# A small tile of 128 bytes becomes one of 512 bytes, and two thirds of the on-chip memory moves up by 384 bytes

## The chip, the cores and the metric

The kernel runs on one core of a Trainium2 chip. The metric is the device time of one launch in microseconds (us). The engines are named as the profile names them: PE is TensorE's matmul, PEld its load of the stationary operand, DVE is VectorE, ACT is ScalarE, POOL is GpSimd and SP is the engine that issues most DMAs. SBUF is the on-chip memory: 128 partitions, in each of which a tile takes the same range of bytes. A byte address below always means the address inside a partition.

## The reference

Pooled attention feeds a gated feed-forward layer.

```python
q, k, v: (8, 8, 576, 64) float32          # batch, heads, sequence, head size
k_p = k.reshape(B, H, 72, 8, D).mean(axis=3)      # 72 pooled keys per head
v_p = v.reshape(B, H, 72, 8, D).mean(axis=3)
scores = (q @ k_p.T) / sqrt(D)
attn = softmax(scores)                            # with 1e-9 added to the sum
x = (attn @ v_p) as (4608 tokens, 512)
gate = sigmoid(x @ w_gate)                        # w_gate, w_val: (512, 1536) float64
out = (gate * (x @ w_val)) @ w_out                # w_out: (1536, 512) float64
```

The weights are float64. The kernel turns them into float32 on the chip and multiplies in three terms: each float32 operand is split into a high part that fits TensorE's one-pass fp32 form and a low rest, and high x high, high x low and low x high are summed in PSUM.

## The kernel before

**Tiling.** The 4608 tokens are nine blocks of 512. Block 0 goes through a first pass of its own, with its order of work written out by hand (`ORDER`, line 264 of the trace). Blocks 1 to 8 go in four pairs, n = 1 to 4, whose order is a list of numbers (`LATER`, line 263). Line numbers of the trace are therefore those of the two loops that issue the work, and tile names tell the operations apart.

**A pair of blocks.** The two matrix products of the feed-forward layer are each cut in 2 x 2 quarters and done with seven products instead of eight. For the first one, seven combinations of x (tiles `xo1` to `xo7`, `parts_of`, line 719) meet seven combinations of the weights (tiles `parts`, reloaded from DRAM into six rotating rooms). `SLOTS` (line 48) fixes the order of 14 products for one pair of weight columns: G1 G5 V4 G6 G2 G3 G7 V1 V5 G4 V6 V2 V3 V7, where V4 belongs to the pair of columns before. The digit says which `xo` is used. Each product is six matmuls, with 512 columns of x streaming through the array (`rhs`) against 128 x 128 of the weights (`lhsT`), `product`, line 772:

```python
t, w, x = bank[kind, b], parts.pop((kind, p, m)), xo[m]
        nc.tensor.matmul(
            t, lhsT=w[:, h, a], rhs=x[:, y, c],
```

The trace calls these matmuls `chain<-xo,parts`. The second product (`second_sums`, line 964) works in the same way on 21 units of 12 matmuls, `acc<-hs,oparts`: `oparts` are reloaded weights in three rotating rooms, and `hs` are combinations of the gated values, which reuse the rooms of the `xo` tiles. The order of these rooms is

```python
ROOMS = (1, 5, 6, 2, 3, 7, 4)
room = ROOMS[i] if i < 7 else (3, 7, 4)[(i - 7) % 3]
```

for the units i = 0 to 20. The attention of the next two blocks (scores `sc`, transposes `tp`, products with v `av`) is threaded between these matmuls in many short pieces.

**The first pass** uses `xo1` and `xo2` for its products (`whole`, line 813: 288 matmuls, trace line 264), and 144 matmuls `acc<-oparts,hs` in which the streaming and the stationary operand are the other way round.

**Where tiles lie.** Tiles come from pools, and a pool lays its rooms one behind the other in SBUF, in the order of their first use. Most tiles are multiples of 512 bytes. A few small ones are rounded up to `LINE` = 32 numbers, 128 bytes:

```python
LINE = 32
zs = work.tile([P, LINE], F32, name="zs")
```

`zs`, the row sums of the softmax, is the first of these in its pool, at byte 74752 = 146 x 512. What follows it starts 128 bytes past a multiple of 512, with few exceptions. In the built program the rooms that matter are:

| room | operand of | before | remainder by 512 | after | remainder |
|---|---|---|---|---|---|
| xo4 | streams x, hs | 12800 | 0 | 12800 | 0 |
| s1 (also an hs) | first pass | 41984 | 0 | 41984 | 0 |
| xo3, xo6, xo7 | streams x, hs | 50176, 58368, 66560 | 0 | the same | 0 |
| xo5, xo1, xo2 | streams x, hs | 76928, 85120, 93312 | 128 | 77312, 85504, 93696 | 0 |
| six rooms of parts | stationary weights | 121984 + 4096 i | 128 | 122368 + 4096 i | 0 |
| three rooms of oparts | stationary weights | 146560 + 4096 i | 128 | 146944 + 4096 i | 0 |

Inside a tile every 512-column operand and every 128 x 128 block starts at a multiple of 512 bytes from the tile's start, so the remainder of the room is that of each operand. By it the 512-column matmuls of one execution fall into two kinds, counted in the built program: in 1404 both operands have the same remainder (1332 of them 128, 72 of them 0, the first pass's `whole` among the former), and in 2064 the remainders differ (1992 with the streaming operand at 0 and the weights at 128, 72 the other way round).

Of the kernel before, what the change touches and what calls it, by code (L numbers as in the profile page):

```python
# [11 lines left out]
F32 = mybir.dt.float32  # L12
# [7 lines left out]
P = 128  # L20
# [11 lines left out]
QT = BT // P  # L32
HT = QT // 2
RING = 5
LINE = 32
# [240 lines left out]
def attention_then_ffn(ctx: ExitStack, tc: tile.TileContext, qT, kT, vm, vr, vn, sums8, wgv, wo, const, out, outT):  # L276
# [3 lines left out]
    def sb(name, bufs=1):  # L280
        return ctx.enter_context(tc.tile_pool(name=name, bufs=bufs))

    cpool, work, two = sb("cpool"), sb("work"), sb("two", 2)
# [20 lines left out]
    def behind(instruction, other):  # L304

        if book.open:
            instruction.behind = other
            return
        link(instruction, other)
# [231 lines left out]
    def load(*what):  # L541
        return fill(rawp.tile([P, S], F32, name="raw"), *what)
# [12 lines left out]
    def prep_k(b, p):  # L555
        ks = work.tile([P, KEYS + LINE - KEYS % LINE], F32, name="ks")[:, :KEYS]
        pool(ks, load("k", b, p), nc.vector)
        i = slot(b, p)
        nc.scalar.activation(kbd[i][:D, :KEYS], ks[:D], AF.Copy, scale=SCALE)
        nc.scalar.activation(kbd[i][D:, KEYS:], ks[D:], AF.Copy, scale=SCALE)  # L560

    def prep_v(b, p, eng):
        vs = work.tile([P, D], F32, name="vs")
        pool(vs, load("v", b, p), eng)
        i = slot(b, p)
        for r in (slice(0, D), slice(D, P)):
            nc.scalar.copy(vh[i][r, r], vs[r])
            eng.tensor_tensor(out=vl[i][r, r], in0=vs[r], in1=vh[i][r, r].bitcast(F32), op=ALU.subtract)

    def prep_vres(b, g, eng):  # L570
        vs = work.tile([P, D], F32, name="vs")[:96]
        pool(vs, load("r", b, g), eng)
        vc = work.tile([96, D], F32R, name="vrc")
        nc.scalar.copy(vc, vs)
        eng.tensor_tensor(out=vc[64:96], in0=vs[64:96], in1=vc[64:96].bitcast(F32), op=ALU.subtract)
        return vc

    def place_vres(b, p, vc):
        for hd in range(2):
            k = p % 2 * 2 + hd  # L580
            nc.scalar.activation(
                vres[slot(b, p)][:, hd * D:hd * D + D], vc.bitcast(F32), AF.Copy, scale=mask[:96, k:k + 1]
            )


    def segments(j):

        t0, cuts = j * BT, []
        t = t0
        while t < t0 + BT:  # L590
            b = t // S
            e = min(t0 + BT, (b + 1) * S)
            cuts.append((t - t0, e - t0, b))
            t = e
        return cuts
# [6 lines left out]
    def room_for_x(j):  # L602
        xs[side(j)] = work.tile([P, NC, BT], F32, name=f"xs{side(j)}")

    def score_matmuls(sc, q, segs, p, hf):
        with book.unit():
            for i in range(HT):
                for a, z, b in segs:
                    t = (hf * HT + i) * P
                    lo, hi = max(a, t), min(z, t + P)  # L610
                    if lo < hi:
                        nc.tensor.matmul(
                            sc[lo - t:hi - t, i], lhsT=q[:, lo:hi], rhs=kbd[slot(b, p)], start=True, stop=True
                        )

    def av_matmuls(av, ph, pl, pr, segs, p):
        for a, z, b in segs:
            i = slot(b, p)
            terms = ((vh[i], ph), (vh[i], pl), (vl[i], ph), (vres[i], pr))
            with book.unit():  # L620
                for k, (w, x) in enumerate(terms):
                    nc.tensor.matmul(av[:, a:z], lhsT=w, rhs=x[:, a:z], start=(k == 0), stop=(k == len(terms) - 1))

    def rest_of(e, rz):

        rest = work.tile([P, 4 * QT, KR], F32, name="rest")
        nc.vector.tensor_tensor(
            out=rest, in0=e.rearrange("p n i k -> p (n i) k")[:, :, KM:],
            in1=rz.rearrange("p n i -> p (n i)")[:, :, None].broadcast_to([P, 4 * QT, KR]), op=ALU.mult,
        )  # L630
        restf = rest.rearrange("p (n i h) k -> p i n (h k)", n=2, h=2)
        r3 = work.tile([P, QT, 3, 4 * KR], F32R, name="r3")
        r3v = [r3[:, :, t].rearrange("p i (n k) -> p i n k", n=2) for t in range(3)]
        nc.vector.tensor_copy(r3v[0], restf)
        end = nc.vector.tensor_tensor(out=r3v[1], in0=restf, in1=r3v[0].bitcast(F32), op=ALU.subtract)
        return (r3v[2], restf), r3, end

    def attention(j, g):
        veng = nc.vector
        segs = segments(j)  # L640
        new = [b for _, _, b in segs if (b, g) not in prepared]
        prepared.update((b, g) for b in new)
        pairs = (2 * g, 2 * g + 1)

        def room_for(shape, name):
            return ps.tile(shape, F32, name=name, tag="sc" if name == "sc" else "tp")

        e = work.tile([P, 2, 2 * QT, KEYS], F32, name="e")
        zs = work.tile([P, LINE], F32, name="zs")[:, :4 * QT].rearrange("p (n i) -> p n i", n=2)
        for n, p in enumerate(pairs):  # L650
            q = load("q", j, p)
            for b in new:
                prep_k(b, p)
            for hf in range(2):
                sc = room_for([P, HT, 2 * KEYS], "sc")
                score_matmuls(sc, q, segs, p, hf)
                scv = sc.rearrange("p i (h k) -> p (i h) k", h=2)
                m = two.tile([P, LINE], F32, name="m")[:, :QT]
                nc.vector.reduce_max(out=m, in_=scv, axis=AX.X, negate=j in BIASED)
                if j in BIASED:  # L660
                    for i in range(QT):
                        nc.scalar.activation(e[:, n, QT * hf + i], scv[:, i], AF.Exp, bias=m[:, i:i + 1])
                else:
                    nc.vector.tensor_tensor(
                        out=e[:, n, QT * hf:QT * hf + QT], in0=scv, in1=m[:, :, None].broadcast_to([P, QT, KEYS]),
                        op=ALU.subtract,
                    )
                yield
        if j not in BIASED:
            nc.scalar.activation(e, e, AF.Exp)  # L670
        nc.vector.reduce_sum(out=zs, in_=e, axis=AX.X)
        nc.vector.tensor_scalar(out=zs, in0=zs, scalar1=EPS, scalar2=float(POOL), op0=ALU.add, op1=ALU.mult)
        rz = work.tile([P, LINE], F32, name="rz")[:, :4 * QT].rearrange("p (n i) -> p n i", n=2)
        nc.vector.reciprocal(out=rz, in_=zs)
        yield
        again, r3, end = rest_of(e, rz)
        nc.scalar.copy(*again)
        tp = room_for([P, BT], "tp")
        tr = tp.bitcast(F32R)
        with book.unit():  # L680
            for i in range(QT):
                nc.tensor.transpose(out=tr[:96, i * P:(i + 1) * P], in_=r3[:, i].rearrange("p t k -> p (t k)"), identity=identr)
        pr = work.tile([96, BT], F32R, name="pr")
        nc.scalar.copy(pr, tp[:96])
        vcs = [(b, prep_vres(b, g, veng)) for b in new]

        def vprep(n, p):
            for b in new:
                prep_v(b, p, veng)
            for b, vc in vcs:  # L690
                place_vres(b, p, vc)

        for n, p in enumerate(pairs):
            pm = work.tile([P, 2 * QT, KM], F32, name="pm")
            behind(nc.gpsimd.tensor_tensor(
                out=pm, in0=e[:, n, :, :KM], in1=rz[:, n, :, None].broadcast_to([P, 2 * QT, KM]), op=ALU.mult
            ), end)
            tp = room_for([P, BT], "tp")
            pmv = pm.rearrange("p (i h) k -> p i (h k)", h=2)
            with book.unit():  # L700
                for i in range(QT):
                    nc.tensor.transpose(out=tp[:, i * P:(i + 1) * P], in_=pmv[:, i], identity=ident)
            ph = work.tile([P, BT], F32R, name="ph")
            pl = work.tile([P, BT], F32R, name="pl")
            nc.scalar.copy(ph, tp)
            nc.vector.tensor_tensor(out=pl, in0=tp, in1=ph.bitcast(F32), op=ALU.subtract)
            vprep(n, p)
            yield
            av = room_for([P, BT], "av")
            av_matmuls(av, ph, pl, pr, segs, p)  # L710
            if p == 0:
                room_for_x(j)
            nc.scalar.copy(xs[side(j)][:, p], av)
            yield
# [695 lines left out]
```

## Time and profile before

| what | value |
|---|---|
| median of 3 runs | 953.01 us (952.88 to 1102.57) |
| the profiled execution | 953.71 us, its span 951.9 us |
| PE busy | 922.8 us, 97% of the span, 4284 matmuls |
| DVE, ACT, POOL busy | 691.1 us, 572.5 us, 70.9 us |
| matmuls `chain` and `acc`, 128x512 | 2028 + 1008 + 288 + 144 = 3468 |
| mean granted TensorE clock | 0.993 |

Matmuls are pipelined: one starts about 230 ns after the one before it, while the profile gives each a length of about 395 ns, from its start to the modelled end of its last column. The step from start to start is what matters for the time. In a row of the timeline or of the chain of waits, a run of n matmuls is merged: in the timeline its length is n - 1 steps and the length of the last matmul, in the chain of waits it is n steps.

### The profile page before, as it was taken

The page shows a single profiled execution, that of the slowest core. Times are in us where ns is not written, and L with a number is a line of the kernel's source. Part 1 is how long each engine was busy: PE and PEld are TensorE (multiplying, and loading weights), DVE is VectorE, ACT ScalarE, POOL GpSimd, SP SyncE. Part 2 cuts the span into 40 slices and gives each one's busy share as a digit, 9 for nine tenths or more (in the row PEclk, how much of TensorE's full clock was granted, in tenths as well). Part 3 has the DMA queues.
Part 4 walks back from the last instruction along what each step waited for, and adds up shares of the span by engine and source line. Part 5 has one row for each costly group of instructions (what it writes and reads, how often), then busy time and mean ns, then how long its engine had stood idle before and what let it go on. Part 6 is the DMA issues. An engine that isn't in the chain of part 4 may idle for free.

```text
span 951.9 us, 12498 instructions
## 1 busy us (share of the span) xinstructions
PE 922.8 (97%) x4284; PEld 749.4 (79%) x4284; DVE 691.1 (73%) x1036; ACT 572.5 (60%) x1041; POOL 70.9 (7%) x95
## 2 busy tenths in 40 slices
PE   5899999999999999999999999999999999999997
PEld 4677878778778888888888878888888888888886
DVE  5999998877879988996439868754478663443853
ACT  6898897698898765674345646652245452233342
POOL 2011110021212100000000000000000100000000
PEclk9899999999999999999999999999999999999999
DMA  9979788757666785699555667556554665554355
GB/s 352 353 236 331 263 323 325 252 182 270 205 249 225 238 252 184 227 321 324 181 194 193 198 229 259 194 168 195 188 178 155 221 229 201 173 202 158 107 180 199
DMA packets 88494, 216.82 MB, mean 228 GB/s; under 512 B 9328, under 2 KB 28016, under 8 KB 86896
## 3 DMA queue, kind: packets, MB, share of 16 engines
q1 hardware_dynamic: 83312, 197.68, 61.2%
q0 software_dynamic: 5120, 18.35, 4.9%
q8 instruction: 34, 0.56, 0.2%
q14 instruction: 28, 0.23, 0.1%
HBM read 165.67 MB, written 50.33 MB: 227 GB/s over the span
## 4 chain that ended last, share of the span: by engine, by line
PE 69%; DVE 6%; ACT 5%; DMA 3%; issue 1%; SPq 0%; DVEq 0%; ACTq 0%
PE chain L263 41%; PE acc L263 22%; PE av L263 2%; PE sc L263 2%; ACT L263 2%; DMA oparts<-keptS 1%; PE tp L263 1%; DVE y L263 1%; DVE s L263 1%; DMA w<-keptwV 1%; DVE parts L263 1%; DMA oparts<-keptO 1%; ACT gate L263 1%; ACT e L263 1%; DVE h L263 1%
## 5 line engine op out<-in xcount | busy, mean ns | idle before, releaser
L263 PE MATMUL chain<-xo,parts 128*128 128x512 f32 x2028 | 486.9, 396 | 2.8 <-DVE o L264 1.9
L263 PEld LDWEIGHTS chain<-xo,parts 128*128 128x128 f32 x2028 | 377.5, 188 | 87.6 <-DVE o L264 2.4
L263 PE MATMUL acc<-hs,oparts 128*128 128x512 f32 x1008 | 247.2, 397 | 2.6 <-DMA oparts<-keptS 2.0
L263 PEld LDWEIGHTS acc<-hs,oparts 128*128 128x128 f32 x1008 | 186.5, 188 | 45.8 <-issue 2.4
L263 DVE TENSOR_TENSOR y<-chain,sV 128x512 f32<-128x512 f32 x69 | 47.4, 689 | 74.0 <-PE chain L263 72.5
L263 ACT COPY sG<-chain 128x512 f32<-128x512 f32 x69 | 40.4, 588 | 99.6 <-PE chain L263 99.5
L263 DVE TENSOR_TENSOR hs<-h,hs 128x1024 fp32r<-128x1024 f32 x48 | 59.4, 1237 | 33.3 <-ACT hs L263 33.2
L263 ACT CAST hs<-h 128x1024 fp32r<-128x1024 f32 x48 | 50.4, 1050 | 43.1 <-PE acc L263 42.3
L263 DVE TENSOR_TENSOR y<-chain,sG 128x512 f32<-128x512 f32 x69 | 47.1, 687 | 34.8 <-ACT gate L263 17.3
L264 PE MATMUL chain<-xo,parts 128*128 128x512 f32 x288 | 69.0, 394 | 0.9 <-DVE parts L264 0.4
L263 ACT ACTIVATE gate<-y 128x512 f32<-128x512 f32 x69 | 43.4, 632 | 37.3 <-DVE y L263 37.0
L264 PEld LDWEIGHTS chain<-xo,parts 128*128 128x128 f32 x288 | 53.3, 188 | 13.8 <-DVE parts L264 1.9
L263 ACT CAST hs<-s 128x1024 fp32r<-128x1024 f32 x36 | 37.8, 1050 | 42.6 <-PE acc L263 22.2
L263 POOL TENSOR_TENSOR pm<-e,rz 128x512 f32<-128x512 f32 x24 | 30.2, 1257 | 433.1 <-PE tp L263 169.6
L263 ACT ACT_TABLE_LOAD x44 | 56.5, 1283 | 8.9 <-DVE e L263 7.9
L263 ACT COPY sV<-chain 128x512 f32<-128x512 f32 x69 | 40.4, 587 | 21.2 <-PE chain L263 20.4
L263 DVE TENSOR_TENSOR hs<-s,hs 128x1024 fp32r<-128x1024 f32 x36 | 46.4, 1288 | 6.3 <-ACT hs L263 6.2
L263 DVE TENSOR_TENSOR h<-y,gate 128x512 f32<-128x512 f32 x69 | 48.2, 701 | 1.7
L263 DVE TENSOR_TENSOR h<-chain,gate 128x512 f32<-128x512 f32 x23 | 15.9, 690 | 39.1 <-PE chain L263 39.1
L264 PE MATMUL acc<-oparts,hs 128*128 128x512 f32 x144 | 36.6, 401 | 0.9 <-DVE oparts L264 0.8
L263 PE MATMUL sc<-kbd,raw 128*128 128x144 f32 (+1 forms) x216 | 33.6, 293 | 0.0
L263 PEld LDWEIGHTS sc<-kbd,raw 128*128 128x128 f32 (+1 forms) x216 | 28.4, 177 | 6.2 <-issue 1.9
(213 smaller groups left out, 1108.2 us busy)
## 6 DMA issues: line engine op xcount, KB each, us to landing
oparts<-keptS SPq DMA_DIRECT2D x48, 512.0 KB, 3.9
oparts<-keptO SPq DMA_DIRECT2D x72, 256.0 KB, 3.5
raw<-in_wgv SPq DMA_DIRECT2D x12, 1024.0 KB, 8.3
out<-o SPq DMA_DIRECT2D x36, 256.0 KB, 4.5
raw<-in_kT SPq DMA_DIRECT2D x28, 288.0 KB, 4.2
raw<-in_qT SPq DMA_DIRECT2D x29, 256.0 KB, 3.8
raw<-in_vm SPq DMA_DIRECT2D x24, 256.0 KB, 3.5
raw_o<-in_wo SPq DMA_DIRECT2D x12, 512.0 KB, 6.7
```

The costliest lines, as they stand in the source:

```text
L263: return self._book.take(lambda: f(*args, **named))
L264: return f(*args, **named)
```

## The change

`zs` in `attention` gets four times `LINE`, 128 numbers or 512 bytes, of which it uses the first 16 numbers as before. Everything that lies behind it in SBUF moves up by 384 bytes, and so the operands of all 512-column matmuls begin at multiples of 512 bytes. The memory's last tile ends at byte 228864 instead of 228480. The number of instructions, their kinds, and their order on each engine stay as they are; only addresses differ.

```diff
         e = work.tile([P, 2, 2 * QT, KEYS], F32, name="e")
-        zs = work.tile([P, LINE], F32, name="zs")[:, :4 * QT].rearrange("p (n i) -> p n i", n=2)
+        zs = work.tile([P, 4 * LINE], F32, name="zs")[:, :4 * QT].rearrange("p (n i) -> p n i", n=2)
         for n, p in enumerate(pairs):
             q = load("q", j, p)
```

## The prediction

> **What bounds the kernel now.** I read the page's busy times first, then busy times by stretch, the waits of PE, the chain of waits, and last the timeline of single runs of matmuls.
>
> ```profile
> span 951.9 us, 12498 instructions
> PE 922.8 (97%) x4284; PEld 749.4 (79%) x4284; DVE 691.1 (73%) x1036; ACT 572.5 (60%) x1041; POOL 70.9 (7%) x95
> L263 PE MATMUL chain<-xo,parts 128*128 128x512 f32 x2028 | 486.9, 396 | 2.8 <-DVE o L264 1.9
> L263 PE MATMUL acc<-hs,oparts 128*128 128x512 f32 x1008 | 247.2, 397 | 2.6 <-DMA oparts<-keptS 2.0
> L264 PE MATMUL chain<-xo,parts 128*128 128x512 f32 x288 | 69.0, 394 | 0.9 <-DVE parts L264 0.4
> L264 PE MATMUL acc<-oparts,hs 128*128 128x512 f32 x144 | 36.6, 401 | 0.9 <-DVE oparts L264 0.8
> ```
>
> PE is busy for 97% of the span, and the four groups of 512-column matmuls, 3468 in all, carry 840 us of its 923. The next view gives busy times by stretch; the columns are the stretch, its length, and for each engine its busy time and number of instructions, then the granted clock and DMA load.
>
> ```profile
> 0.00:60.00 60.00, 45.69 (x211) 36.37 (x212) 47.85 (x87) 48.35 (x117) 7.25 (x23) 0.91 0.92 327
> 60.00:300.00 240.00, 231.49 (x1100) 186.44 (x1099) 207.79 (x349) 208.84 (x406) 38.57 (x53) 0.99 0.73 263
> 300.00:500.00 200.00, 199.56 (x953) 163.38 (x952) 152.53 (x231) 113.34 (x212) 12.37 (x9) 1.00 0.70 239
> 500.00:700.00 200.00, 198.85 (x943) 163.14 (x942) 135.69 (x204) 101.02 (x172) 8.77 (x8) 1.00 0.62 202
> 700.00:880.00 180.00, 180.00 (x798) 146.59 (x798) 104.14 (x127) 74.50 (x107) 3.96 (x3) 1.00 0.57 190
> ```
>
> From 300 us on PE is idle for less than 1%, while DVE and ACT have room. The waits of PE after 300 us, with their sum, number and longest, say the same:
>
> ```profile
> PE acc L263 <- DMA oparts<-keptS: 2.0, 2, 1.2
> PE acc L263 <- ACT vh L263: 0.3, 1, 0.3
> ```
>
> So after 300 us the time is the number of matmuls times the step from one start to the next. Before 300 us DVE and ACT are busy for 87% and PE loses 8.5 us after the first 60: a mixed bound.
>
> **What the step depends on.** The change moves addresses alone, so the question is whether a step depends on them. The kernel itself holds the experiment, since its operands stand in all four combinations of remainders by 512. Four runs of 18 matmuls each, from the timeline of PE (start, length, count); nothing interrupts them:
>
> ```profile
> 68.00 4.25 PE L264 MATMUL acc<-oparts,hs 128*128 128x512 f32 x18
> 885.95 4.24 PE L263 MATMUL acc<-hs,oparts 128*128 128x512 f32 x18
> 121.11 4.36 PE L264 MATMUL acc<-oparts,hs 128*128 128x512 f32 x18
> 900.43 4.36 PE L263 MATMUL acc<-hs,oparts 128*128 128x512 f32 x18
> ```
>
> By the table of addresses, the first has both operands at remainder 0 and the second both at 128; the third streams from 128 against weights at 0, the fourth from 0 against weights at 128. A length is 17 steps and one last matmul of about 0.39 us (the groups' means are 394 to 401 ns). That makes (4.25 - 0.39) / 17 = 227.1 and 226.5 ns where the remainders agree, 226.8 on average, and 233.5 ns where they differ: 6.7 ns more, whichever operand is the one off. Being at 0 is not what matters; being alike is. After the change all are alike, at 0, which is the first row's case.
>
> The Trainium skill, page "TensorE: Matmul & The Clock Gate", section "Back-to-back issue gap", gives the gap of a warm stream as N / 2.4 + 2.5 ns, without any term for an address. By it 512 columns would be 216 ns in all four rows and the change would save nothing; the rows differ from it and from each other, so the rows decide.
>
> **The change part by part.** It removes and adds no instruction and moves none on any engine. The chain of waits shows what the steps are in longer runs; here a length is n full steps.
>
> ```profile
> 430.15 70.65 PE chain L263 x306
> 639.01 62.38 PE chain L263 x270
> 774.63 110.79 PE chain L263 x480
> 895.07 27.93 PE acc L263 x120
> 504.84 4.12 PE acc L263 x18
> 333.09 5.58 PE acc L263 x24
> ```
>
> *Unbroken runs.* The first three rows are 1056 matmuls in 243.82 us, 230.9 ns each: the list of slots has 8 unequal products to 6 equal ones, and a switch between them costs the first steps of an equal one a little. All equal, they go at 226.8: 1056 x 4.1 ns = 4.3 us. The fourth row is 232.75 ns a step, with 108 of 120 unequal: 120 x 5.95 ns = 0.7 us. Together 5.0 us.
>
> *Broken runs.* Elsewhere pieces of attention interrupt the stream, and after each break some steps are slow whatever the addresses. The last two rows are runs after a break: 228.9 ns all equal, 232.5 ns all unequal, 3.6 ns apart. Of the 2064 unequal matmuls 8/14 x 1056 = 603 and 108 are counted already, which leaves 1353: x 3.6 ns = 4.9 us. The bounds are 0 (if a break resets everything) and the full 6.7 ns, 9.1 us. I take the 3.6 since these rows are of that very kind.
>
> *What is given back.* Before 300 us lie 312 of the unequal matmuls (72 of the first pass, 24 of its last columns, and 4.5 of the first pair's five groups of columns at 48), worth 312 x 3.6 ns = 1.1 us. DVE and ACT are at 87% there and several waits of PE end on them, so I count half as lost: 0.6 us, rounded up. The two DMA waits of 2.0 us can grow by what PE gains while a load is under way, two units or 24 matmuls at 6.7 ns, 0.16 us each: 0.3 us.
>
> *Other operands that move.* The scores' streamed and stationary tiles had unequal remainders mostly and keep them so (the key tiles lie at 192 to 448, unmoved; the rooms of q move from 384, 128, 384 to 256, 0, 256). There are 160 of these matmuls in the program, and at 6.7 ns either way they are worth at most 1.1 us; I take 0. DVE, ACT and DMA addresses move from one multiple of 128 to another. No row separates that for them; after 300 us their cover is PE itself, which waits 2.3 us for all of them together, so a per cent on DVE's 392 us of work between 300 and 880 us would be hidden. If that cover were gone, 1% of it would be 4 us, either way; I take 0.
>
> Sum: 5.0 + 4.9 - 0.6 - 0.3 = 9.0 us. The profiled execution took 953.7 us (span 951.9 and 1.8 around it), so 944.7 for it; it stands 0.7 above the median of the runs, 953.0, from which I predict **944.0 us**, 0.9% less.
>
> **The rivals.**
>
> *No change, 953 us.* The steps would follow from something that goes with the rooms and not from the remainder, such as which tiles were just written by DVE or DMA. For it: the equal rooms are always xo1, xo2, xo5, the same use in every round. Against it: the first and third timeline rows are the same loop of the first pass, with the same kind of operands, and differ in remainder alone, and the third has the opposite operand at 128 from the fourth. The Trainium skill, page "SBUF — State Buffer", section "A bandwidth-pool intuition that's wrong (but worth ruling out)", says that PE's load of weights has a second, independent read port, so that the two streams could not disturb each other wherever they lie; if that held, this rival would be the outcome. The four rows speak against it.
>
> *Half absorbed, about 949 us.* The gain of the broken runs is lost because the attention between them is paced by DVE and ACT, not by PE. Then only the unbroken 5.0 us less 0.3 remain: 953.0 - 4.7 = 948.3. For it: DVE at 76% in the stretch from 300 to 500. Against it: PE idle of 0.4 us in those 200.
>
> *Slower: the clock.* A denser stream of matmuls could make the chip grant PE less clock between 300 and 950 us. The clock does fall in this trace, once in the steady part, after PE was idle for 1.9 us (the columns are as above, the clock third from the end):
>
> ```profile
> 170.46 5.79 PE L263 MATMUL chain<-xo,parts 128*128 128x512 f32 x17 [1.93 <-DVE o L264]
> 171.50:175.00 3.50, 3.50 (x10) 2.72 (x9) 1.84 (x3) 0.00 (x0) 0.00 (x0) 0.53 0.46 177
> ```
>
> That was idleness, not load; a stretch like it costs 1.6 us (3.5 us at about half). Under load the rows from 300 to 880 us show 1.00, equal runs included. To be slower than 953 the 650 us after 300 would have to lose more than the 9.0 us gained: a mean clock under 0.986. At 0.95 it would be 944 + 34 = 978 us. The Trainium skill, page "TensorE: Matmul & The Clock Gate", section "What's actually happening" and the warning behind "Seeing it yourself", has the clock at half after idleness, and at 13/16 under load only once three cores of a die are busy. By that rule the one core here would not be throttled, and the rows from 300 to 880 us agree.
>
> **How the numbers follow.** Forecast (the steps become equal and most of the gain reaches the end, 940 to 947): 0.77. Half absorbed, 947 to 951: 0.10. No change, 951 to 955: 0.07. Slower by the clock: 0.03. A gain over 2%, under 934 us, would need a step below 221 ns, which no row shows: 0.03. The lower end takes the dear bound for the broken runs: 5.0 + 9.1 - 0.3 = 13.8, or 939.2, rounded in to 940 since the part before 300 us can't give all; the upper end reaches into the absorbed case, 949.5. About 2% is what a measurement of this kernel can tell from no change, and by that bound: faster 0.03, within 0.94, slower 0.03.
>
> **What would show it.** Each step: runs of 18 uninterrupted matmuls are 4.24 or 4.25 us wherever they stand, the two at 4.36 among them. The long runs of `chain` in the chain of waits come to 226.8 ns a matmul, the one of 480 to 108.9 us instead of 110.79. The group of 2028 keeps its count and its mean falls from 396 ns to about 391. PE's busy time falls by about 9 us, and its idle time, 29 us of the span, grows by less than 1 us. Wrong would be: the unequal runs still at 4.36 (the first rival); steps of 227 with PE's idle time up by 4 us or more (the second); a clock under 1.00 after 300 us (the third). The median is wrong above 949.5 or below 940.

## The result and the profile after

The median went from 953.2 to 943.9 us. One run of the kernel before, 1102.57 us, was a slow one, and the ratio of the mean times is taken without it: 0.9909 with a 95% interval of 0.9894 to 0.9924, 0.9% faster and clear of noise. The prediction was 944.0 us with a range of 940.0 to 949.5. The profiled execution took 944.9 us, 8.8 less than the one before.

The page's totals and groups of matmuls with the change (busy time, mean of one, idle time before them):

```profile
span 943.1 us, 12498 instructions
PE 911.2 (97%) x4284; PEld 748.1 (79%) x4284; DVE 689.3 (73%) x1036; ACT 572.3 (61%) x1041; POOL 67.4 (7%) x95
L263 PE MATMUL chain<-xo,parts 128*128 128x512 f32 x2028 | 479.1, 392 | 2.9 <-DVE o L264 2.0
L263 PE MATMUL acc<-hs,oparts 128*128 128x512 f32 x1008 | 243.6, 394 | 3.4 <-DMA oparts<-keptS 2.5
L264 PE MATMUL chain<-xo,parts 128*128 128x512 f32 x288 | 69.1, 394 | 0.9 <-DVE parts L264 0.4
```

The two groups of the steady part lost 7.8 and 3.6 us. The group of 288, whose operands agreed before as well, did not move (69.0 to 69.1 us), and DVE and ACT hardly did (1.8 and 0.2 us less in all). POOL's 3.5 us less are one instruction of its 95: a product `pm<-e,rz` that took 4.57 us at 308.50 us before and 1.04 at 307.91 with the change.

The same four runs of 18 matmuls with the change, from the timeline of PE, in the order in which the prediction shows them; the last two were at 4.36:

```profile
69.49 4.27 PE L264 MATMUL acc<-oparts,hs 128*128 128x512 f32 x18
877.62 4.24 PE L263 MATMUL acc<-hs,oparts 128*128 128x512 f32 x18
122.60 4.26 PE L264 MATMUL acc<-oparts,hs 128*128 128x512 f32 x18
891.22 4.24 PE L263 MATMUL acc<-hs,oparts 128*128 128x512 f32 x18
```

And the chain of waits with the change, for the runs that carried the sum (430.15, 639.01, 774.63 and 895.07 before), with the two rows at which the traces part first and last:

```profile
171.91 8.45 PE chain L263 x36
428.37 69.42 PE chain L263 x306
634.96 61.30 PE chain L263 x270
768.31 108.80 PE chain L263 x480
886.63 27.33 PE acc L263 x120
931.09 8.44 PE acc L263 x36
```

These two of before belong to the first and the last:

```profile
170.46 10.15 PE chain L263 x36
939.71 8.62 PE acc L263 x36
```

The difference of the starts measures the gain so far. At the first row the changed kernel is 1.45 us behind: it lost that in the first 60 us, where its PE was busy for 44.12 us instead of 45.69 (the stretch is shown below); one profile of each kernel can't tell whether the change has a share in that. The run of 36 in this row is 1.70 us shorter, which is nearly all the clock and not the change: before, PE ran 3.4 us of it at half clock, and this time it did not. From there on, ahead by 0.25 us, the changed kernel gains 1.5 until 428 us, 2.3 until 635, 2.3 until 768 and 2.1 until 887, 0.2 more until 931 and the last 0.2 in that row: 8.55 us from the end of the run of 36, at 180 us, to the end of the kernel.

### The profile page after: what moved, and what is told of

Same layout as the page of the kernel before. It is cut to its first block, busy times and chain, and to the rows that moved or that the text cites. A ratio compares the mean times of both kernels' runs of the same rounds, so it can differ in the third digit from the quotient of the medians.

```text
span 943.1 us, 12498 instructions
## 1 busy us (share of the span) xinstructions
PE 911.2 (97%) x4284; PEld 748.1 (79%) x4284; DVE 689.3 (73%) x1036; ACT 572.3 (61%) x1041; POOL 67.4 (7%) x95
## 4 chain that ended last, share of the span: by engine, by line
PE 67%; DVE 6%; ACT 5%; DMA 4%; issue 1%; SPq 0%; DVEq 0%; ACTq 0%
PE chain L263 42%; PE acc L263 20%; PE av L263 2%; ACT L263 2%; PE sc L263 2%; DMA oparts<-keptS 2%; PE tp L263 1%; DMA w<-keptwV 1%; DVE hs L263 1%; ACT e L263 1%; DMA oparts<-keptO 1%; ACT gate L263 1%; DVE y L263 1%; DMA raw<-in_vr 1%; DVE parts L263 0%
## 5 line engine op out<-in xcount | busy, mean ns | idle before, releaser
L263 PE MATMUL chain<-xo,parts 128*128 128x512 f32 x2028 | 479.1, 392 | 2.9 <-DVE o L264 2.0
L263 PE MATMUL acc<-hs,oparts 128*128 128x512 f32 x1008 | 243.6, 394 | 3.4 <-DMA oparts<-keptS 2.5
L264 PE MATMUL chain<-xo,parts 128*128 128x512 f32 x288 | 69.1, 394 | 0.9 <-DVE parts L264 0.4
L263 POOL TENSOR_TENSOR pm<-e,rz 128x512 f32<-128x512 f32 x24 | 26.6, 1110 | 431.3 <-PE tp L263 165.1
```

Source lines behind the costliest of these rows:

```text
L263: return self._book.take(lambda: f(*args, **named))
L264: return f(*args, **named)
```

## The experiments

Three theories stood against each other. The prediction's: a step is short when the streamed operand and the weights begin alike by 512 bytes, wherever that is. The one that the change's description suggests: an operand has to begin at a multiple of 512. The rival of the prediction: the steps go with the rooms and their use. Each ratio is against runs of the kernel before on the same chip; the first four experiments share one chip and the last two another.

### All operands alike, but off

```diff
-cst = cpool.tile([P, P + 16], F32, name="cst")
+cst = cpool.tile([P, P + 16 + LINE], F32, name="cst")     # with the change
```

> The change, and a constant tile in front of everything made 128 bytes longer: all operands of the 512-column matmuls now begin 128 bytes past a multiple of 512, alike but none at 0. Alike is enough: 943.9 us as with the change (942 to 946), uninterrupted runs of 18 matmuls at 4.24 or 4.25 us. Being at a multiple of 512 is what counts: every operand is off, so at least the time before, 953 us, with runs of 18 at 4.36 us.

Measured: 943.2 us, ratio 0.9902 (0.9887 to 0.9918). The run of 18 that was at 4.36 us before, and the run of 480 in the chain of waits:

```profile
893.22 4.24 PE L263 MATMUL acc<-hs,oparts 128*128 128x512 f32 x18
770.30 108.80 PE chain L263 x480
```

No operand of the 512-column matmuls begins at a multiple of 512 here, and the time and the steps are those of the change. The multiple does nothing by itself.

### All weights off, all streamed operands at 0

```diff
-m = two.tile([P, LINE], F32, name="m")[:, :QT]
+m = two.tile([P, LINE + LINE // 2], F32, name="m")[:, :QT]     # two buffers: 128 bytes; with the change
```

> The change, and a small tile pair between the x rooms and the weights made 128 bytes longer in all: x and hs at remainder 0, all weights at 128, so 3324 of the 3468 chain and acc matmuls are unequal instead of 2064 before and none with the change. Alike is what counts: the cost goes with the count, (953.2 - 943.9) / 2064 = 4.5 ns each, so 943.9 + 3324 x 4.5 ns = 958.9 us (956 to 962), runs of 18 at 4.36 us in xo1 and xo2 as well. Only the place of the streamed operand counts: 944 us, as with the change. The rooms and their use are what counts: 953 us, as before.

Measured: 956.7 us, ratio 1.0037 (1.0025 to 1.0049): slower than before, in the expected range and below its middle. A run of 18 in the room xo1 and xo5, at 4.24 us before, and the run of 480:

```profile
886.92 4.35 PE L263 MATMUL acc<-hs,oparts 128*128 128x512 f32 x18
774.84 111.55 PE chain L263 x480
```

Rooms that were fast are slow once their partner is moved, which ends the theory of the rooms. (The edit moves the reloaded weights and what lies behind them in SBUF; the 144 matmuls `acc<-oparts,hs` of the first pass stay equal.) The cost doesn't go strictly with the count, though: the run of 480 lost 2.75 us against the change with all 480 unequal, 5.7 ns each, and in the kernel before 1.99 us with 275 unequal, 7.2 ns each. The kernel before paid also for switching between the two kinds. When each start in its trace is matched with the operands' addresses in the built program, the 275 unequal matmuls of that run come to 232.6 ns a step, and the 205 equal ones to 228.4: 229.2 for the first six after a switch to their kind, and 226.7, as with the change, for the rest.

### 256 bytes apart

```diff
-zs = work.tile([P, LINE], F32, name="zs")
+zs = work.tile([P, 2 * LINE], F32, name="zs")
```

> The kernel before with the small tile at 256 bytes instead of 128: the same 2064 matmuls are unequal, their operands now 256 bytes apart by 512. Alike by 512 bytes: 953 us as before, unequal runs of 18 at about 4.36 us. Alike by 256 bytes is enough: 944 us, all runs of 18 at 4.24 or 4.25 us. A cost that grows with the distance, doubled: 944 + 18.6 = 962 us.

Measured: 945.3 us, ratio 0.9916 (0.9901 to 0.9931), whose interval overlaps that of the change. The unequal run at the end and the run of 480:

```profile
891.15 4.24 PE L263 MATMUL acc<-hs,oparts 128*128 128x512 f32 x18
768.23 108.80 PE chain L263 x480
```

Operands 256 bytes apart are as fast as operands alike by 512. The prediction's period of 512 was twice too long, which its trace, with distances of 0 and 128 alone, couldn't show. A cost that only grows with the distance is out.

### 64 bytes apart

```diff
-zs = work.tile([P, LINE], F32, name="zs")
+zs = work.tile([P, 4 * LINE + 16], F32, name="zs")
```

> The change with 64 bytes more in the small tile: the same 2064 matmuls as before are unequal, their operands 64 bytes apart by 512. Any distance costs the same: 953 us, unequal runs of 18 at about 4.36 us. A cost in proportion to the distance of 64 bytes: half of 9.3 us, 948.6 us. A distance below 128 bytes costs nothing: 944 us.

Measured: 954.3 us, ratio 1.0018 (1.0006 to 1.0030). The unequal run at the end, streaming from 0 against weights at 64; the unequal run of the first pass, streaming from 64 against weights at 0; and the run of 480:

```profile
898.48 4.36 PE L263 MATMUL acc<-hs,oparts 128*128 128x512 f32 x18
121.52 4.29 PE L264 MATMUL acc<-oparts,hs 128*128 128x512 f32 x18
773.04 111.10 PE chain L263 x480
```

Half the distance costs the whole price, and slightly more than before. But the first pass's run, with the operands the other way round, is cheaper: 4.29. The next two runs were made for that sign, and for a distance shorter still.

### 192 bytes apart

```diff
-zs = work.tile([P, LINE], F32, name="zs")
+zs = work.tile([P, 4 * LINE + 48], F32, name="zs")
```

> The change with 192 bytes more in the small tile: the same 2064 matmuls as before are unequal, 1992 of them streaming from 192 bytes below the weights by 512, which is 64 above them by 256. If the distance counts by 256 and with its sign, as the 72 reversed matmuls of the run with 64 bytes hint (about 229.4 ns a step where the other 1992 took 233.3): 943.9 + 1992 x 2.3 ns = 948.5 us (947 to 950), uninterrupted unequal runs of 18 at 4.28 to 4.30 us. If every distance that is no multiple of 256 costs the same: 953 to 954 us, runs of 18 at 4.36 us.

Measured: 950.5 us, ratio 0.9977 (0.9965 to 0.9989), outside both expected ranges and nearer to the first. The same three rows:

```profile
897.31 4.28 PE L263 MATMUL acc<-hs,oparts 128*128 128x512 f32 x18
121.92 4.36 PE L264 MATMUL acc<-oparts,hs 128*128 128x512 f32 x18
772.37 110.63 PE chain L263 x480
```

The two runs of 18 changed places against the run with 64 bytes, as the sign demands. The size came out too small because I priced the unequal matmuls alone: the run of 480 is at 110.63 / 480 = 230.5 ns, above the 228.8 ns of (4.28 - 0.39) / 17. Matched with the addresses as above, its 205 equal matmuls come to 231.1 ns a step, and its 275 unequal ones to 231.0 for the first six after a switch to their kind and 228.9 for the rest: mixing the two kinds makes both slow.

### 32 bytes apart

```diff
-zs = work.tile([P, LINE], F32, name="zs")
+zs = work.tile([P, 4 * LINE + 8], F32, name="zs")
```

> The change with 32 bytes more in the small tile: the same 2064 matmuls are unequal, 1992 of them streaming from 32 bytes below the weights by 512. If every distance that is no multiple of 256 costs the same: 953 to 954 us, unequal runs of 18 at 4.36 us. If the cost begins at 64 bytes: 944 us, runs at 4.24 or 4.25 us. If it is in proportion to the distance up to 64 bytes: half, 948 to 949 us.

Measured: 953.9 us, ratio 1.0014 (1.0005 to 1.0024). Both unequal runs:

```profile
898.82 4.36 PE L263 MATMUL acc<-hs,oparts 128*128 128x512 f32 x18
121.89 4.36 PE L264 MATMUL acc<-oparts,hs 128*128 128x512 f32 x18
```

A distance of 32 bytes costs the full price in either direction.

Taken together, by the distance of the streamed operand above the weights, modulo 256 bytes:

| distance | run of 18, us | step, ns | from |
|---|---|---|---|
| 0 | 4.24 to 4.27 | 227 to 228 | the change, all at 128, 256 apart |
| 32 | 4.36 | 233 | 32 apart, first pass |
| 64 | 4.28, 4.29 | 229 | 192 apart; 64 apart, first pass |
| 128 | 4.34 to 4.36 | 233 | before; weights at 128 |
| 192 | 4.36 | 233 | 64 apart; 192 apart, first pass |
| 224 | 4.36 | 233 | 32 apart |

Step is the length less 0.39 us, by 17. The lower price of 64 is that of runs of one kind; in the run of 480, which mixes the kinds, 64 bytes cost nearly what the kernel before paid (110.63 us against 110.79, and 108.80 with the change). What in the memory or in PE makes these numbers isn't settled: that the two operands' places matter together is shown, a mechanism is not. Distances of 96 and 160 bytes, those that are no multiple of 32, other widths and other types were not tried. Nothing here points to a version faster than the change: with all operands alike the long runs are at 226.7 ns (108.80 / 480) in three kernels that place them differently.

## Why the prediction was right

*What bounds the kernel.* PE, as read; the steps went down and the time followed. Its busy time fell by 11.6 us, of which some 1.7 are the half clock of the execution before at 172 us, and its idle time rose from 29.1 to 31.9 us, more than the "less than 1 us" that was written. Of these 2.8 us 1.6 lie in the first 60, 0.5 between 60 and 300, and 0.8 after 300, where the DMA waits grew by 1.1 (below) and a wait of 0.3 for ACT is gone. The mean of the 2028 was put at 391 ns and is 392.

*What the step depends on.* Alike and not at 0: shown by the run with all operands at 128. The remainder that counts is that by 256, not 512; for the change, where both are met, it made no difference.

*Unbroken runs, 5.0 us.* Measured 1.23 + 1.08 + 1.99 + 0.60 = 4.9 us, from the four rows. The run of 480 was put at 108.9 and took 108.80.

*Broken runs and what is given back, 4.9 - 0.6 - 0.3 = 4.0 us.* What the 8.55 us leave beside the 4.9 of the unbroken runs is 3.65 us. The two traces, matched matmul by matmul from 180 us on, split it: 1268 of the 1353 unequal matmuls outside the four rows took 4.4 us less, 3.5 ns each where the prediction had 3.6; equal ones and the pieces of attention took 0.4 less; and PE was idle for 1.2 us more, where the prediction had 0.9 given back. The DMA waits grew from 2.0 to 3.1 us (the two rows below), by 1.1 us instead of 0.3:

```profile
PE acc L263 <- DMA oparts<-keptS: 2.5, 3, 1.4
PE acc L263 <- DMA oparts<-keptO: 0.6, 1, 0.6
```

*Other operands, 0.* With all rooms moved by 128 again the time was 943.2, and with other places of the q rooms 945.3: within 1.4 us of the change, so in these placements what DVE, ACT, DMA and the scores gain or lose by their addresses is no more than that.

*The rivals.* "No change" fell with the runs of 18 in the changed kernel. "Half absorbed" fell with PE's idle time after 300 us: the stretches of 200 us show PE busy for 199.59 and 198.68, as before.

```profile
0.00:60.00 60.00, 44.12 (x204) 35.67 (x205) 46.37 (x84) 46.80 (x116) 7.25 (x23) 0.94 0.89 320
60.00:300.00 240.00, 231.03 (x1109) 186.76 (x1108) 209.40 (x352) 210.59 (x408) 38.89 (x53) 1.00 0.73 264
300.00:500.00 200.00, 199.59 (x967) 165.39 (x966) 154.29 (x235) 115.51 (x214) 8.50 (x9) 1.00 0.72 242
500.00:700.00 200.00, 198.68 (x951) 164.67 (x951) 137.49 (x206) 102.44 (x174) 9.82 (x9) 1.00 0.63 203
700.00:880.00 180.00, 180.00 (x808) 149.07 (x807) 106.63 (x131) 75.55 (x107) 2.91 (x2) 1.00 0.56 187
```

In the same 580 us PE now starts more matmuls (967, 951 and 808 against 953, 943 and 798). "Slower by the clock" fell with the 1.00 in these rows. The step "below 221 ns" that the prediction sets for a gain over 2% is too low: 9 of the 19 us are in the equal steps already, and the 10 us from 944 to 934 over 3468 matmuls are 2.9 ns, so about 224 ns would do; no row shows that either.

The prediction weighed two statements that spoke for no change. In the Trainium skill, page "TensorE: Matmul & The Clock Gate", section "Back-to-back issue gap", the gap of N / 2.4 + 2.5 ns has no term for an address. That section of the Trainium skill calls it the gap of an isolated matmul, though the same page also has it for matmuls back to back, as the prediction does, and gives about 131 ns for a sustained stream of 512 columns. The steps here, 227 to 233 ns, meet neither the 131 nor the formula's 216. In the Trainium skill, page "SBUF — State Buffer", section "A bandwidth-pool intuition that's wrong (but worth ruling out)", the load of weights has a second, independent read port. That the two streams could therefore not disturb each other was the prediction's conclusion. Against it, moving the weights and what lies behind them by 128 bytes cost 12.8 us (943.9 to 956.7).

*What was luck.* The forecast of 944.0 and the median of 943.9 agree to 0.1 us by luck. Single runs of the changed kernel spread from 942.95 to 945.22 us, and in the two profiles 1.45 us lost at the start and 1.70 won by the clock, neither of them in the sum, happen almost to cancel. What the runs bear out is the step, the count and the gain of about 9 us.

## What to carry to other kernels

When PE is busy all the time, read the step from start to start in uninterrupted runs, and compare runs whose operands lie in different rooms: a kernel can hold such an experiment already, and the count of each kind then gives the size of the gain. For matmuls of this kind, place the streamed operand and the weights alike by 256 bytes; a small tile allocated between them can put them apart, and padding it costs bytes and no instruction. Check where a gain lands with the starts of the same rows in both chains of waits, since start-up and the clock can hide or feign a microsecond or two.

## What was not expected of the hardware

The period of 256 bytes, and the sign: in runs of one kind a distance of 64 bytes costs about a third of what 32, 128, 192 or 224 cost (4.28 against 4.36 us for 18, where alike is 4.24). And the clock: after the same wait at about 170 us (1.93 us idle before, 1.96 with the change) PE fell to half clock for 3.4 us before the change and stayed at full clock with it. The rows of the changed kernel, to be held against those of the prediction's third rival:

```profile
171.91 4.37 PE L263 MATMUL chain<-xo,parts 128*128 128x512 f32 x18 [1.96 <-DVE o L264]
171.50:175.00 3.50, 3.09 (x14) 2.56 (x15) 3.28 (x4) 0.32 (x2) 0.00 (x0) 1.00 0.93 358
```

Of the six experiments the one with all operands at 128 fell to half clock at this place too (a granted clock of 0.75 in the same 3.5 us), and the other five did not (1.00); no placement goes with that. The length of the idle time alone, to which the prediction put the half clock down, doesn't decide it; what does is open.
